# Moving the result's store to ScalarE, and the first load ahead of SyncE's base-address read

## The chip, the cores and the metric

The kernel runs on one core of one Trainium2 chip. The metric is the device time of one execution, in microseconds (us). Before the change it was 188.28 us (median of 3 runs, 188.20 to 188.41). A run's time is about 1.3 us longer than the span that its profile shows (187.95 against 186.69 us in the profiled run of before), because the span counts only from the first to the last recorded instruction of the kernel.

Names of engines: PE is TensorE's matmul, PEld its weight load, DVE is VectorE, ACT is ScalarE, POOL is GpSimd, SP is SyncE. "SPq" and "ACTq" are the sequencers of SyncE and ScalarE, which issue DMAs.

## The reference, cut

One decode step for 2 batch rows of 640 features: attention over the last 1024 entries of a 4096-entry cache (32 heads of 192), then a gated feed-forward block, both modulated by vectors made from `c`.

```python
mod = (_silu(c) @ w_mod).reshape(c.shape[0], 6, 1, -1)
sa, ca, ga, sb, cb, gb = (mod[:, i].copy() for i in range(6))   # written out in the original
h = _layernorm(x, axis=-1) * (1 + ca) + sa
x = x + ga * _A_ref(h, A_k_cache, A_v_cache, A_wq, A_wo)
h = _layernorm(x, axis=-1) * (1 + cb) + sb
x = x + gb * _B_ref(h, B_w_gate, B_w_up, B_w_down)
return x                                                        # (2, 1, 640) bf16: 2.5 KB
```

It reads 76.9 MB and writes 2.5 KB.

## The kernel before

All work is written as operations with reads and writes, and a small scheduler turns these into semaphore waits. Every weight and cache load is issued by SyncE, in the order of use. Two places matter here.

The end. The result lies in 8 rows of `finb`, 16 partitions apart (four chunks of 160 features, times two batch rows). SyncE stores them, and then waits for the store to land:

```python
S.op("pe", f, ..., name="down%d" % ci)               # last matmuls, per landed piece of w_down
S.op("dve", ... fin = ps * modR[:, 5], name="gb_y")
S.op("dve", ... finb = fin + X, name="outR")
S.dma("sp", k_dma(out[:, 0, :].rearrange("b (i n) -> i b n", i=NR), finb[0:P:RB, :]),
      sem_out, reads=["finb"], name="st_out")
# ... cut ...
S.emit("sp", nc.sync, tail=lambda e: e.wait_ge(sem_out, 16))
```

The beginning. A program starts with a preamble (zeroing of registers, a read of the core's base address into two registers on each engine, constants on GpSimd) and a barrier of all engines, which for each engine is a drain and a wait. The kernel before already lifts its first load, of `w_mod`, out of the body and puts it directly in front of SyncE's drain:

```python
body = nc.main_func.blocks[0].instructions
entry = next(i for i, x in enumerate(body) if x.opcode == "Drain" and x.engine == mybir.EngineType.SP)
first = S.lists["sp"].pop(0)                          # the load of w_mod
# ... cut: an assert ...
n0 = len(body)
first.fn(nc.sync).then_inc(first.sem, first.inc)
moved = body[n0:]
del body[n0:]
body[entry:entry] = moved
```

## Time and profile before

| what | value |
|---|---|
| time, span | 188.28 us, 186.7 us |
| chain of work that ended last | 72% DMA, 16% VectorE |
| DMA engines' busy share, each fortieth of the span | 8 to 9 tenths, all but the last |
| first load issued, second load issued | 0.00 and 0.79 us |
| end of outR to end of the span | 1.78 us |

From the page of the kernel before: the span, the row of DMA busy shares in tenths over 40 slices, and the chain's shares by engine.

```profile
span 186.7 us, 2408 instructions
...
DMA  8989998999999999999999999999999999999991
...
DMA 72%; DVE 16%; PE 5%; ACT 2%; SPq 1%; issue 1%
```

The DMA engines are busy for 80% or more of every slice until the last. This is a kernel that streams its weights and caches. Nothing at its two ends can matter unless it moves the whole stream (the head) or what follows the stream (the tail).

The timeline of before at the head. The columns are start (us), duration (us), engine, line, operation, output and input, count, and in brackets the idle time before it and what ended that.

```profile
0.00 0.39 SPq L266 DMA_DIRECT2D r<-in_w_mod_dram  x1
0.29 0.10 POOL L724 MEMSET const-float32-0.0<- 128x1 f32 x1 [0.29 <-issue]
...
0.79 0.81 SPq L266 DMA_DIRECT2D ring<-in_A_wq_dram  x2
```

The first load is the first thing recorded. The memset on GpSimd belongs to the preamble, and the load starts 0.295 us ahead of it. The second load comes after the barrier.

The timeline of before at the tail.

```profile
183.54 0.64 PE L684 MATMUL ps<-r,aT 128*17 128x160 bf16 x16 [0.65 <-DMA r<-in_B_w_down_dram]
...
184.23 0.33 DVE L689 TENSOR_TENSOR fin<-ps,modR 128x160 f32<-128x160 f32 x1 [2.73 <-PE ps L684]
184.59 0.33 DVE L691 TENSOR_TENSOR finb<-fin,X 128x160 bf16<-128x160 f32 x1
184.94 0.69 SPq L266 DMA_DIRECT2D out_dram<-finb  x1
```

And the waits of SyncE's queue in before: who waited for whom, us in total, times, the longest.

```profile
SPq L266 <- DVE finb L691: 23.3, 1, 23.3
...
SPq L706 <- DMA out_dram<-finb: 1.0, 1, 1.0
```

The last piece of `w_down` lands, 16 matmuls finish the product, two VectorE operations make the result, and then come 0.69 us of issuing and 1.0 us of waiting for 2.5 KB. No other work is left at that time, so this 1.7 us is wholly on the critical path.

### The profile page before, as it was taken

How to read it: one execution, taken by the hardware profiler on the slowest of the kernel's cores; microseconds unless marked ns; L12 is line 12 of the kernel's file. 1: busy time of each engine (PE TensorE's matmuls, PEld its weight loads, DVE VectorE, ACT ScalarE, POOL GpSimd, SP SyncE). 2: the span in 40 equal slices, each digit the busy share in tenths (PEclk: the TensorE clock that was granted, in tenths of full speed). 3: DMA queues.
4: the chain of work that ended last, by engine and by line, in shares of the span. 5: the costliest groups of instructions: out<-in, count | busy, mean ns of one | idle time of the engine just before them, and what ended most of it. 6: DMA issues, size and time to landing. Idle time of an engine off the chain costs nothing.

```text
span 186.7 us, 2408 instructions
## 1 busy us (share of the span) xinstructions
PE 106.9 (57%) x1038; PEld 51.9 (28%) x1039; DVE 98.2 (53%) x147; ACT 30.0 (16%) x72; POOL 5.1 (3%) x23
## 2 busy tenths in 40 slices
PE   0015710833876678656649656665576895356472
PEld 0011200211243333322314313333233252355321
DVE  6114000019788889587596595785865934002311
ACT  2022100091020212021012011110110103100610
POOL 8200000000000000000000000000000000000000
PEclk9999999997899999999996999999998558555567
DMA  8989998999999999999999999999999999999991
GB/s 296 486 366 437 474 422 379 437 427 427 429 424 427 417 426 432 424 424 425 421 427 427 427 430 421 420 429 424 429 422 424 449 462 422 404 402 428 408 399 51
DMA packets 6518, 77.03 MB, mean 413 GB/s; under 512 B 746, under 2 KB 876, under 8 KB 1516
## 3 DMA queue, kind: packets, MB, share of 16 engines
q1 hardware_dynamic: 6492, 76.88, 97.6%
q8 instruction: 8, 0.13, 0.3%
q14 instruction: 2, 0.02, 0.0%
q10 hardware_dynamic: 16, 0.01, 0.0%
HBM read 76.88 MB, written 0.00 MB: 412 GB/s over the span
## 4 chain that ended last, share of the span: by engine, by line
DMA 72%; DVE 16%; PE 5%; ACT 2%; SPq 1%; issue 1%
DMA ring<-in_A_k_cache_dram 38%; DMA ring<-in_A_wq_dram 17%; DMA r<-in_B_w_down_dram 17%; DVE prod L490 10%; DVE S_sb L509 4%; PE ps L502 2%; PE ps L467 2%; ACT qbc L483 2%; SPq L266 1%; DVE ps L485 1%; DVE M L512 1%; ACT qrow L474 1%; DVE bcR L519 0%; PE ps L526 0%; PE ps L684 0%
## 5 line engine op out<-in xcount | busy, mean ns | idle before, releaser
L490 DVE TENSOR_TENSOR prod<-ring,qbc 128x3072 bf16<-128x3072 bf16 x32 | 55.9, 1752 | 16.1 <-DMA ring<-in_A_k_cache_dram 16.1
L502 PE MATMUL ps<-prod,ident_b 128*128 128x512 bf16 x192 | 51.5, 411 | 15.7 <-DVE prod L490 15.6
L502 PEld LDWEIGHTS ps<-prod,ident_b 128*128 128x128 bf16 x192 | 17.2, 102 | 40.3 <-DVE prod L490 21.0
L509 DVE TENSOR_REDUCE S_sb<-ps 128x32 f32<-128x1024 f32 x16 | 19.3, 1206 | 0.9 <-PE ps L502 0.9
L526 PE MATMUL ps<-bcR,bcL 5*128 5x4 f32 x32 | 6.3, 264 | 22.3 <-DVE bcR L519 22.3
L563 ACT ACTIVATE On<-ps,rden 128x384 bf16<-128x384 f32 x16 | 9.3, 581 | 42.4 <-DVE rden L561 31.9
L551 PE MATMUL ps<-ring,E_sb 128*8 128x384 bf16 x256 | 14.8, 356 | 0.0
L534 ACT ACTIVATE E_sb<-Sb_sb 128x128 bf16<-128x128 f32 x16 | 5.0, 311 | 57.6 <-DVE Sb_sb L531 57.6
L467 PE MATMUL ps<-ring,hT 128*2 128x512 bf16 x60 | 6.7, 626 | 9.9 <-DMA ring<-in_A_wq_dram 9.0
L526 PEld LDWEIGHTS ps<-bcR,bcL 5*128 5x128 f32 x32 | 4.9, 190 | 26.3 <-DVE bcR L519 26.3
L622 PE MATMUL ps<-ring,oT 128*17 128x160 bf16 x192 | 6.8, 338 | 5.5 <-DMA ring<-in_A_wo_dram 5.5
L477 DVE CAST qrow<-ps 128x512 bf16<-128x512 f32 x1 | 0.7, 692 | 15.8 <-PE ps L467 15.8
L531 DVE TENSOR_TENSOR Sb_sb<-S_sb,ps 128x128 f32<-128x128 f32 x16 | 4.6, 289 | 7.8 <-PE ps L526 7.8
L540 PEld LDWEIGHTS ps<-denp,maskc 128*128 128x128 f32 x32 | 6.9, 218 | 3.6 <-ACT E_sb L534 0.9
L622 PEld LDWEIGHTS ps<-ring,oT 128*17 128x17 bf16 x192 | 6.1, 135 | 6.1 <-DMA ring<-in_A_wo_dram 6.1
L641 DVE TENSOR_TENSOR lnt<-ps,modR 128x160 f32<-128x160 f32 x1 | 0.3, 325 | 13.6 <-PE ps L622 13.6
L551 PEld LDWEIGHTS ps<-ring,E_sb 128*8 128x8 bf16 x256 | 5.0, 87 | 3.2 <-issue 0.7
L467 PEld LDWEIGHTS ps<-ring,hT 128*2 128x2 bf16 x60 | 1.7, 114 | 14.9 <-DMA ring<-in_A_wq_dram 9.9
L540 PE MATMUL ps<-denp,maskc 128*128 128x1 f32 x32 | 5.0, 226 | 0.8 <-ACT E_sb L534 0.8
L383 PE MATMUL ps<-ident_b,crow 2*128 2x2 bf16 x5 | 0.4, 177 | 8.2 <-DMA crow<-in_c_dram 8.2
L576 PE MATMUL ps<-On,zsel 128*128 128x96 bf16 x64 | 4.6, 223 | 0.7 <-ACT On L563 0.7
L514 PE MATMUL ps<-ident_f,M 128*1 128x128 f32 x16 | 4.5, 280 | 0.4 <-DVE M L512 0.4
(81 smaller groups left out, 71.5 us busy)
## 6 DMA issues: line engine op xcount, KB each, us to landing
ring<-in_A_k_cache_dram SPq DMA_DIRECT2D x16, 1536.0 KB, 24.6
ring<-in_A_v_cache_dram SPq DMA_DIRECT2D x16, 1536.0 KB, 24.8
r<-in_w_mod_dram SPq DMA_DIRECT2D x1, 4800.0 KB, 14.1
ring<-in_A_wq_dram SPq DMA_DIRECT2D x1, 4608.0 KB, 32.0
ring<-in_A_wo_dram SPq DMA_DIRECT2D x1, 4480.0 KB, 24.6
ring<-in_A_wq_dram SPq DMA_DIRECT2D x1, 3072.0 KB, 20.6
ring<-in_A_wo_dram SPq DMA_DIRECT2D x1, 2720.0 KB, 23.0
r<-in_B_w_gate_dram SPq DMA_DIRECT2D x1, 1920.0 KB, 25.1
```

Source lines behind the costliest of these rows:

```text
L467: last = e.matmul(ps[32 * i:32 * i + B, n, :], lhsT=hT[:, k, :], rhs=wv[:, kk, i, n * QW:(n + 1) * QW], start=(k == 0), stop=(k == KT - 1) ...
L490: S.op("dve", lambda e: e.tensor_tensor(out=prod[:, 2 * (g % 2) + ci, :, :], in0=ring[:, sl, ci * JC * Dh:(ci + 1) * JC * Dh].rearrange("p ...
L502: last = e.matmul(o_ap, lhsT=ident_b[:, :], rhs=prod[:, pz, :, t * GC:(t + 1) * GC], start=(t == 0), stop=(t == NCH - 1))
L509: S.op("dve", lambda e: e.tensor_reduce(out=S_sb[:, z, :], in_=ps[:, 2 * z:2 * z + 2, :].rearrange("p k (j c) -> p (k j) c", c=GC), axis=A ...
L526: S.op("pe", lambda e: e.matmul(ps[:, BK_T, P:P + HQ], lhsT=bcL[:, :], rhs=bcR[:, z, :], start=True, stop=True), reads=[("bcR", z), "bcL"] ...
L531: S.op("dve", lambda e: e.tensor_tensor(out=Sb_sb[:, z, :, :], in0=S_sb[:, z, :].unsqueeze(2).broadcast_to([P, J, HQ]), in1=ps[:, BK_T, P: ...
L534: S.op("act", lambda e: e.activation(out=E_sb[:, z, :, :], in_=Sb_sb[:, z, :, :], func=ACTF.Exp, scale=SCALE, accum_out=denp[:, z:z + 1]), ...
L540: S.op("pe", lambda e: e.matmul(ps[:, BK_T, P + 16:P + 17], lhsT=maskc[:, :], rhs=denp[:, z:z + 1], start=True, stop=True), reads=[("denp" ...
L551: last = e.matmul(ps[32 * i:32 * i + 2 * HQ, BK_O, 0:ON], lhsT=E_sb[:, z, 2 * jp:2 * jp + 2, :].rearrange("p j h -> p (j h)"), rhs=ring[:, ...
L563: S.op("act", lambda e: e.activation(out=On[:, quad % 2, b, :], in_=ps[:, BK_O, 0:ON], func=ACTF.Identity, scale=rden[:, z:z + 1]), reads= ...
L576: last = e.matmul(ps[:, BK_OT, 0:B * NT].rearrange("p (b t) -> p b t", b=B), lhsT=zsel[:, jj, x:x + P], rhs=On[:, quad % 2, :, jj * Dh + d ...
L622: last = e.matmul(ps[32 * i:32 * i + RM, BK_M, 0:DR], lhsT=oT[:, t, :], rhs=wv[:, tl, i, :], start=(t == 0), stop=(t == NT - 1), tile_posi ...
```

## The change

Its intent: ScalarE is idle at the end and could issue the store faster or sooner; and the very first load should not wait for the base-address read.

```diff
-        S.dma("sp", k_dma(out[:, 0, :].rearrange("b (i n) -> i b n", i=NR), finb[0:P:RB, :]),
+        S.dma("act", k_dma(out[:, 0, :].rearrange("b (i n) -> i b n", i=NR), finb[0:P:RB, :]),
               sem_out, reads=["finb"], name="st_out")
 
         S.resolve()
         body = nc.main_func.blocks[0].instructions
-        entry = next(i for i, x in enumerate(body) if x.opcode == "Drain" and x.engine == mybir.EngineType.SP)
+        own = [i for i, x in enumerate(body) if x.engine == mybir.EngineType.SP]
+        entry = next(i for i in own if body[i].opcode == "Drain")
+        base = next(i for i in own if body[i].opcode == "ISA")
+        assert base < entry
+        body.insert(entry - 1, body.pop(base))
+        entry -= 1
```

In the source, SyncE's order becomes: first load, base-address read, drain. It was: base-address read, first load, drain.

## The prediction

> **What bounds the kernel now.** The page: span 186.7 us (that run took 187.95; median 188.28). Its row of DMA busy shares is 8 or 9 tenths in every slice but the last; the chain that ended last is 72% DMA. So it is a streaming kernel, and this change touches only its two ends.
>
> Head (timeline): SyncE issues the w_mod load at 0.00, the next load at 0.79, after the entry barrier; w_mod has landed at 14.1 and PE uses it at 14.16. A real advance of the first load could save as much as it advances, since everything queues behind it.
>
> Tail (timeline and DMA packets): the last w_down load lands at 183.5, the last matmuls end at 184.2, outR ends at 184.91, SyncE issues the store from 184.94 to 185.63, its packets run at 186.23 to 186.33, the last completion increment is at 186.66, SyncE's final wait is over at 186.68. The store's issue and landing, 1.72 us, lie wholly on the critical path.
>
> **The entry part.** The base-address read is an instruction of the common preamble that writes two registers. Nothing in this program reads them. In the compiled program of the kernel before, SyncE's stream holds no such read: the w_mod load is its first kernel instruction, then the drain and the barrier's wait. The unused read is dropped on compiling, and should be dropped wherever it stands. I expect a stream equal to the one before, and 0.00 us here. If the read did survive, moving it would be worth at most its own duration, which the trace does not show.
>
> **The store.** Removed: SyncE's issue, 694 ns. Added: the same issue on ScalarE, 8 rows of 320 bytes. The trace has a near twin: ScalarE's load of x, the same shape the other way, 630 ns; its first completion count (written when issuing is done) came 1.06 us after the issue began, the store's on SyncE 1.07 us. Waking on VectorE takes ScalarE 33 to 36 ns, SyncE 27 to 29: +6 ns. ScalarE is idle from 178.4, SyncE from 161.6, so nothing is freed. SyncE still waits for the store to land. The Trainium skill, "DMA: Bandwidth & Descriptors", section "Issuing engines are not separate DMA queues", says that issuing elsewhere saves only sequencer time and that all transfers share 16 engines; the trace agrees: ScalarE's two small loads at the head, issued at 0.80 and 1.40, landed at 8.2 and 12.5, behind SyncE's packets. At the tail the DMA engines are empty. Unknown: from issue's end to first packet SyncE's store took 0.60 us; for ScalarE's queue, idle since 12 us, there is no clean figure. Sum: -0.06 to +0.2 us, about +0.02.
>
> **Prediction.** 188.25 us, 187.85 to 188.7 at 8 in 10 (mostly spread between executions and chips). Faster by over 2%: 0.005; within 2%: 0.985; slower by over 2%: 0.01.
>
> **What would show it.** First load at 0.00, SyncE's second load at about 0.79, PE's mod matmuls at about 14.2; the store issued by ScalarE about 35 ns after outR, for 0.60 to 0.72 us, on the queue that carried c and x; end of outR to end of span 1.65 to 1.95 us (before: 1.78).
>
> **What would make it wrong.** The read survives and costs some tenths at the start; ScalarE's long idle queue starts late; ScalarE's end-of-program work, now begun about 7 us later, outlasts SyncE's final wait and lengthens the time outside the span (1.26 us in the profiled run).

## The result, and the profile after

| | before | after |
|---|---|---|
| median | 188.16 us (6 runs, 187.88 to 188.41) | 188.21 us (6 runs, 188.14 to 188.32) |
| span of the profiled run | 186.69 us | 186.89 us |
| its time less its span | 1.257 us | 1.256 us |

The ratio is 1.0004, with a 95% interval of 0.9991 to 1.0017: the same. (A ratio here and below is the mean time of one kernel's fast runs over that of the other's of the same rounds, so it is not quite the ratio of the medians quoted beside it.)

The page of after, the same three lines.

```profile
span 186.9 us, 2409 instructions
...
DMA  9989999999999999999999999999999999999991
...
DMA 72%; DVE 16%; PE 6%; ACT 2%; SPq 1%; issue 1%
```

The timeline of after at the head.

```profile
0.00 0.37 SPq L266 DMA_DIRECT2D r<-in_w_mod_dram  x1
0.29 0.10 POOL L729 MEMSET const-float32-0.0<- 128x1 f32 x1 [0.29 <-issue]
...
0.79 0.80 SPq L266 DMA_DIRECT2D ring<-in_A_wq_dram  x2
```

Nothing has moved: the first load is 0.295 us ahead of the memset, exactly as before. The reason is seen in the compiled program. This is SyncE's stream from its start, in before and in after alike:

```
DMACopy         r3 <- w_mod
Drain           (entry barrier)
EventSemaphore  (entry barrier)
DMACopy         ring <- wq
```

There is no base-address read in either. Nothing in the program reads the two registers that it fills, and it is dropped when the program is built. Instruction by instruction, SyncE's two compiled streams differ in one thing: the store at the end is gone.

The timeline of after at the tail, and the wait of SyncE's queue for the store.

```profile
184.47 0.33 DVE L689 TENSOR_TENSOR fin<-ps,modR 128x160 f32<-128x160 f32 x1 [2.78 <-PE ps L684]
184.83 0.33 DVE L691 TENSOR_TENSOR finb<-fin,X 128x160 bf16<-128x160 f32 x1
185.19 0.60 ACTq L266 DMA_DIRECT2D out_dram<-finb  x1
```

```profile
SPq L711 <- DMA out_dram<-finb: 25.3, 1, 25.3
```

The store is now ScalarE's, 0.09 us shorter to issue. SyncE's wait has grown from 1.0 to 25.3 us, which looks alarming and costs nothing: SyncE had nothing else to do, and it used to spend the first 23.3 us of that time waiting for VectorE instead. (This shows why a sum of waits is no measure of cost. What counts is when the last one ends.)

The tail in detail, from the instruction, packet and semaphore records of the trace, in us after the end of outR:

| | issue starts | issue lasts | first completion count | first packet | last completion count | span ends |
|---|---|---|---|---|---|---|
| before (SyncE) | 0.028 | 0.694 | 1.100 | 1.321 | 1.747 | 1.780 |
| after (ScalarE) | 0.033 | 0.603 | 1.058 | 1.273 | 1.708 | 1.741 |

ScalarE wakes 5 ns later, issues 91 ns shorter, and its first packet then follows 0.637 us after the end of the issue in place of 0.599: the gain is 39 ns of 188 us. The span of this after run is nevertheless 0.20 us longer, all of it between the memset and the end of outR, where the two programs do the same; between executions of one program that stretch varies as much (store_only, below, compiles to the same program as after, byte for byte, and its span is 0.31 us shorter; entry_only compiles to that of before and its span is 0.11 us longer).

The first completion count is worth a look. The Trainium skill, "DMA: Bandwidth & Descriptors", section "Why a DMA increments its semaphore by 16 and not by 1", says that such a transfer uses k of 16 DMA engines, k being the largest number up to 16 that divides the slowest dimension of both sides, and that the sequencer writes the missing 16 - k at once while each used engine adds one when its data has landed. This store's dimensions are 8 on one side and 4 on the other, so k should be 4, and the trace agrees: until the span's end its semaphore has five updates, in before as in after: one early, and about 0.6 us later four within 45 to 49 ns.

### The profile page after: what moved, and what is told of

Same layout as the page of the kernel before. It is cut to its first block, busy times and chain, and to the rows that moved or that the text cites. A ratio compares the mean times of both kernels' runs of the same rounds, so it can differ in the third digit from the quotient of the medians.

```text
span 186.9 us, 2409 instructions
## 1 busy us (share of the span) xinstructions
PE 105.3 (56%) x1039; PEld 51.3 (27%) x1039; DVE 98.0 (52%) x147; ACT 29.9 (16%) x72; POOL 5.1 (3%) x23
## 4 chain that ended last, share of the span: by engine, by line
DMA 72%; DVE 16%; PE 6%; ACT 2%; SPq 1%; issue 1%
DMA ring<-in_A_k_cache_dram 38%; DMA ring<-in_A_wq_dram 17%; DMA r<-in_B_w_down_dram 17%; DVE prod L490 10%; DVE S_sb L509 4%; PE ps L502 2%; PE ps L467 2%; ACT qbc L483 2%; SPq L266 1%; DVE ps L485 1%; DVE M L512 1%; PE ps L526 0%; DVE bcR L519 0%; PE ps L684 0%; ACT qrow L474 0%
## 5 line engine op out<-in xcount | busy, mean ns | idle before, releaser
L502 PE MATMUL ps<-prod,ident_b 128*128 128x512 bf16 x192 | 49.2, 396 | 16.3 <-DVE prod L490 16.2
L445 PE MATMUL ps<-r,scT 128*17 128x480 bf16 x40 | 4.3, 598 | 2.1 <-DMA r<-in_w_mod_dram 2.1
L519 DVE TENSOR_REDUCE bcR<-ps 1x4 f32<-1x128 f32 x16 | 4.3, 272 | 0.8 <-PE ps L514 0.8
## 6 DMA issues: line engine op xcount, KB each, us to landing
r<-in_B_w_gate_dram SPq DMA_DIRECT2D x1, 1920.0 KB, 25.3
```

Source lines behind the costliest of these rows:

```text
L502: last = e.matmul(o_ap, lhsT=ident_b[:, :], rhs=prod[:, pz, :, t * GC:(t + 1) * GC], start=(t == 0), stop=(t == NCH - 1))
```

## The experiments

My theory: the entry part compiles to nothing; the store's issue and landing are on the critical path, but cost the same to within 0.1 us on either engine. Rivals: (a) the two parts each move time and cancel; (b) the head or the tail has slack, so that such changes could not matter; (c) ScalarE's later finish lengthens the end of the program. Rival (c) is answered by the result itself: the time outside the span is 1.257 us before and 1.256 us after in the profiled runs.

### 1. Each part alone

Two kernels, `entry_only` (the diff without its store line) and `store_only` (the store line alone).

> Only the entry part of the change. The compiled program is byte for byte that of the kernel before. Mine: a null test, within 0.15 us of the kernel before, and any difference is the spread between executions. Rival (the entry part gains something and the store gives it back): faster by 0.2 us or more, the first load earlier against the first memset than the 0.29 us of before.

> Only the store moved to ScalarE. Mine: within 0.15 us of before; from the end of outR to the end of the span 1.70 to 1.80 us (before 1.78, with both parts 1.74). Rival (the two parts cancel): slower by 0.2 us or more, with a longer time outside the span than 1.26 us.

`entry_only`: 188.12 us against 188.27, ratio 0.9996 (0.9983 to 1.0010). The first load lies 0.294 us ahead of the memset, and the end of outR to the end of the span is 1.782 us. As the compiled programs are byte for byte the same on all five engines, this is what no change looks like: two medians 0.15 us apart.

`store_only`: 188.03 us, ratio 0.9993 (0.9980 to 1.0005). The end of outR to the end of the span is 1.745 us, its issue 0.612 us, close to the changed kernel. Its tail:

```profile
184.51 0.33 DVE L691 TENSOR_TENSOR finb<-fin,X 128x160 bf16<-128x160 f32 x1
184.87 0.61 ACTq L266 DMA_DIRECT2D out_dram<-finb  x1
```

So the parts do not cancel (rival a): one is nothing and the other is 0.04 us. That figure comes from the traces, where five runs with the old store show 1.776 to 1.792 us and two with ScalarE's show 1.741 and 1.745; the times alone cannot resolve it.

### 2. The base-address read, kept alive

What would the entry part be worth if the read did run? One instruction that stores its register into an unused word, placed where SyncE idles, keeps it in the program. `live_ahead` adds this to the kernel before, `live_behind` to the kernel with the entry part.

```diff
+        junk = sb("junk", [1, 2], mybir.dt.int32)
...
+        keep = _Op("sp", lambda e: e.reg_save(junk[0:1, 0:1], e.tpb_base_reg.lo), "keep_base")
+        S.lists["sp"].insert(len(S.lists["sp"]) - 1, keep)      # ahead of the store
```

(The function that emits the operations also got three lines that emit this one without a semaphore.)

> The base-address read is kept in the program by one later store of its register into an unused word (issued while SyncE idles), and it stands ahead of the first load, as the source of the kernel before has it. Mine: the read now runs, delays the first load by its own duration d, and the whole program by d, since all loads queue behind the first: slower than before by d, which I estimate at 0.05 to 0.6 us; the first load comes later against the first memset than in before. Rival (the head has slack): the first load is later but the time is the same.

> The same live read, standing behind the first load, as the changed source has it. Mine: within 0.15 us of before, faster than live_ahead by nearly all of d, as the read hides behind the first load's transfer; the second load may come later by d without cost. Rival (the read costs the same wherever it stands, as the second load and the entry barrier follow it): as slow as live_ahead.

The timeline of live_ahead at the head.

```profile
0.06 0.38 SPq L270 DMA_DIRECT2D r<-in_w_mod_dram  x1
0.28 0.10 POOL L730 MEMSET const-float32-0.0<- 128x1 f32 x1 [0.28 <-issue]
...
0.84 0.81 SPq L270 DMA_DIRECT2D ring<-in_A_wq_dram  x2
```

And of live_behind.

```profile
0.00 0.39 SPq L270 DMA_DIRECT2D r<-in_w_mod_dram  x1
0.29 0.10 POOL L735 MEMSET const-float32-0.0<- 128x1 f32 x1 [0.29 <-issue]
...
0.84 1.07 SPq L270 DMA_DIRECT2D ring<-in_A_wq_dram  x2
```

Now the trace holds the read, an instruction recorded as a base load: at 0.000 us in live_ahead, with the first load 64 ns later, and at 0.457 us in live_behind. In live_ahead the load is 0.215 us ahead of the memset in place of 0.295. Placed behind, the load is back at 0.293 and it is the barrier that is late: the second load stands 0.55 us after the memset in place of 0.50. That costs nothing visible, since the DMA engines have w_mod's 4800 KB to move until about 14 us.

The times: live_ahead 188.31 us, ratio 1.0007 (0.9995 to 1.0020); live_behind 188.24 us, ratio 1.0003 (0.9990 to 1.0015). Both are the same as before; 0.06 to 0.08 us is at the lower edge of what I had expected and too little for the times to show. So the order of the first load and the read is worth at most 0.08 us even in a program in which the read exists. That the total gains this much from moving it stays argued, not measured.

### 3. Does the head have slack?

`late_first` leaves out the lifting altogether: the first load is an ordinary instruction after the barrier (the nine lines from `body = ...` on are deleted).

> The first load is issued after the entry barrier, not ahead of it. In before it starts 0.29 us ahead of the first memset on GpSimd; here it should start 0.35 to 0.50 us after that memset, a delay of 0.64 to 0.79 us. Mine (everything queues behind the first load, so the head is fully on the critical path): slower than before by 0.6 to 0.8 us, ratio 1.003 to 1.0045. Rival (the head has slack, which is why the entry part did nothing): within 0.15 us.

Its timeline at the head.

```profile
0.30 0.10 POOL L715 MEMSET const-float32-0.0<- 128x1 f32 x1 [0.30 <-issue]
...
0.80 0.39 SPq L266 DMA_DIRECT2D r<-in_w_mod_dram  x1
...
1.25 0.88 SPq L266 DMA_DIRECT2D ring<-in_A_wq_dram  x2
```

The load starts 0.492 us after the memset in place of 0.295 ahead of it: 0.787 us later. The second load, behind it on SyncE, starts 0.45 us later than in before. The time is 188.97 us against 188.30, ratio 1.0033 (1.0020 to 1.0045), which is 0.62 us of 188.3. So the head has no slack worth speaking of (rival b falls there), and the first load's place is a real lever. The kernel before had pulled it already; the change had nothing left to pull.

### 4. Does the tail have slack?

The store cut in two, one per batch row, both issued by ScalarE (`split_act`), or one by SyncE and one by ScalarE (`split_sp_act`):

```diff
-        S.dma("sp", k_dma(out[:, 0, :].rearrange("b (i n) -> i b n", i=NR), finb[0:P:RB, :]),
-              sem_out, reads=["finb"], name="st_out")
+        for bb, eng in ((0, "act"), (1, "act")):                 # split_sp_act: "sp" for row 0
+            S.dma(eng, k_dma(out[bb, 0, :].rearrange("(i n) -> i n", i=NR), finb[RB * bb:RB * bb + 97:32, :]),
+                  sem_outs[bb], reads=["finb"], name="st_out%d" % bb)
...
-        S.emit("sp", nc.sync, tail=lambda e: e.wait_ge(sem_out, 16))
+        S.emit("sp", nc.sync, tail=lambda e: [e.wait_ge(s, 16) for s in sem_outs])
```

> The store is cut in two, one for each batch row, both issued by ScalarE one after the other; SyncE waits for both. Mine (the issue of the store is fully on the critical path): a second issue of about 0.6 us is added, end of outR to end of span 2.3 to 2.45 us against 1.74 with one store on ScalarE, and slower than before by 0.5 to 0.65 us. Rival (issuing overlaps with the landing, so its engine and its length do not matter): within 0.15 us.

> The same two stores, one issued by SyncE and one by ScalarE at the same time. Mine: the issue is mostly a fixed cost, so each half takes about 0.6 us and the two run side by side: end of outR to end of span 1.65 to 1.80 us, within 0.15 us of before. If the issue scaled with the rows it would be 1.4 us and 0.3 us faster. Rival (two issuing engines get in each other's way): 2.0 us or more.

The tail of split_act (two issues merged in one line).

```profile
184.95 0.32 DVE L691 TENSOR_TENSOR finb<-fin,X 128x160 bf16<-128x160 f32 x1
185.31 1.11 ACTq L266 DMA_DIRECT2D out_dram<-finb  x2
```

Two issues of 0.568 and 0.512 us follow each other, and the end of outR to the end of the span grows to 2.242 us, 0.50 us more than with one store on ScalarE. The time is 188.78 us against 188.30, ratio 1.0021 (1.0009 to 1.0034), or 0.40 us (0.17 to 0.64). A little less than I had expected, since the halves are shorter to issue, but clear: the tail has no slack either (rival b falls there too).

The tail of split_sp_act.

```profile
184.81 0.32 DVE L691 TENSOR_TENSOR finb<-fin,X 128x160 bf16<-128x160 f32 x1
185.16 0.66 SPq L266 DMA_DIRECT2D out_dram<-finb  x1
185.16 0.57 ACTq L266 DMA_DIRECT2D out_dram<-finb  x1
```

Here my expectation failed. The two issues start within 4 ns of each other and look parallel. ScalarE's half lands as it does alone (first count 1.02, last 1.66 us after outR). SyncE's half has its first count at 1.38 us and its last at 2.01 us, with an issue of 0.657 us that is not longer than usual. The span ends 2.03 us after outR, later than with one store (1.78). The time is 188.50 us, ratio 1.0008 (0.9996 to 1.0021), the same within the noise. Against the same two halves issued one after the other (split_act, 2.24 us), issuing at once did save 0.21 us, but that is far from the 0.60 us by which the second issue there starts after the first. So the two issues seem to have got in each other's way somewhere between the sequencers and the DMA engines, after the recorded issue; the order of the two first packets (ScalarE's at 1.25, SyncE's at 1.60 us, on engines otherwise idle) suggests that it was not the DMA engines. What they share there, these runs do not show, and this is one trace; no run issues SyncE's half alone (its whole stores with this partition step, in six traces, have their first count at 1.09 to 1.12 us).

### 5. If not the engine, the shape

The trace of before has issues of two lengths on SyncE. Where its queue is not full, plain two-dimensional loads take 0.33 to 0.43 us, the cache loads and the store 0.53 to 0.69 us (0.63 and more at the head and for the store). On ScalarE, the load of x takes 0.63 us, and the plain load of c 0.55. (The expectation below says 0.61 to 0.69 us for the long ones; most of the cache loads take 0.53 to 0.54.) `rows_flat` stores 8 neighbouring partitions in plain order. Its result is wrong (the result does not lie there); the bytes and rows are as many.

```diff
-        S.dma("sp", k_dma(out[:, 0, :].rearrange("b (i n) -> i b n", i=NR), finb[0:P:RB, :]),
+        S.dma("sp", k_dma(out[:, 0, :].rearrange("b (i n) -> (b i) n", i=NR), finb[0:2 * NR, :]),
               sem_out, reads=["finb"], name="st_out")
```

> A deliberately wrong result: SyncE stores the first 8 partitions, whose addresses form a plain two-dimensional block on both sides, in place of the 8 rows that lie 16 partitions apart. Same bytes, same rows. The trace has two lengths of issue: 0.33 to 0.43 us for plain two-dimensional loads, 0.61 to 0.69 us for those with a third dimension. Mine: the issue takes 0.33 to 0.43 us, end of outR to end of span 1.40 to 1.55 us, faster than before by 0.2 to 0.35 us: the shape of the store is worth more than its engine. Rival: the issue is as long as before, 0.6 us or more, and the time the same.

Its tail.

```profile
184.84 0.33 DVE L691 TENSOR_TENSOR finb<-fin,X 128x160 bf16<-128x160 f32 x1
185.20 0.37 SPq L266 DMA_DIRECT2D out_dram<-finb  x1
```

The issue takes 0.368 us in place of 0.694, and the first packet follows 0.421 us after it in place of 0.599. The end of outR to the end of the span is 1.286 us, 0.49 us less than before and more of a gain than I had expected (1.40 to 1.55). The time is 187.70 us against 188.30, ratio 0.9966 (0.9952 to 0.9979), which is 0.64 us (0.40 to 0.90). The 0.49 us of the tail are more than ten times what the engine is worth there.

Which property of the shape does it? `stride_rows` (also wrong) keeps two plain dimensions and 8 rows on both sides, but reads `finb[0:P:RB, :]` again, 16 partitions apart.

> A deliberately wrong result: the store reads the 8 rows 16 partitions apart, as before, but writes them to the output in plain order, so both sides have two dimensions and only the partition step is left of what made the store different from rows_flat. Mine: the compiler marks rows_flat's store for the shorter issue and not this one, so the issue is 0.6 to 0.7 us again and the end of outR to the end of the span 1.65 to 1.80 us. Rival (the third dimension of the output side, or 8 rows shared out over 8 DMA engines in place of 4, made rows_flat short): 1.25 to 1.45 us.

```profile
184.75 0.32 DVE L691 TENSOR_TENSOR finb<-fin,X 128x160 bf16<-128x160 f32 x1
185.10 0.71 SPq L266 DMA_DIRECT2D out_dram<-finb  x1
```

The issue is 0.714 us, the first packet 0.597 us after it, the end 1.805 us after outR, the time 188.11 us (ratio 0.9999, 0.9987 to 1.0012). So neither the third dimension nor the number of DMA engines used (both wrong-result stores have nine semaphore updates, which is k = 8) makes the store short. With two plain dimensions on both sides, neighbouring partitions do. (They are not enough alone: the cache loads write 128 neighbouring partitions, have a third dimension on the other side, and are long.) In the compiled programs the short store and all of SyncE's short loads carry a mark for a prepared form of issue, and the long ones do not. (ScalarE's load of c carries it too and still took 0.55 us, so the mark does not explain every length.)

### 6. A correct version with the short store

`gather` pays for neighbouring partitions with a matmul. A 0/1 matrix gathers the 8 rows of gb*y, rounded to bf16 here, into partitions 0 to 7, in the output's order; X is gathered in the same way earlier, beside the stream.

```diff
-        fin = sb("fin", [P, DR], F32)
-        finb = sb("finb", [P, DR], BF16)
+        fin = sb("fin", [P, DR], BF16)
+        finb = sb("finb", [B * NR, DR], BF16)      # also new: selo, selof (0/1, made on GpSimd), Xg
...
+        S.op("pe", lambda e: e.matmul(ps[0:B * NR, 3, 0:DR], lhsT=selof[:, :, :].rearrange("p b i -> p (b i)"), rhs=X[:, :], ...
+        S.op("dve", lambda e: e.tensor_copy(out=Xg[:, :], in_=ps[0:B * NR, 3, 0:DR]), ...      # both after the gate matmuls
...
-        S.op("dve", lambda e: e.tensor_tensor(out=finb[:, :], in0=fin[:, :], in1=X[:, :], op=ALU.add), ...
-        S.dma("sp", k_dma(out[:, 0, :].rearrange("b (i n) -> i b n", i=NR), finb[0:P:RB, :]), ...
+        S.op("pe", lambda e: e.matmul(ps[0:B * NR, 3, 0:DR], lhsT=selo[:, :, :].rearrange("p b i -> p (b i)"), rhs=fin[:, :], ...
+        S.op("dve", lambda e: e.tensor_tensor(out=finb[:, :], in0=ps[0:B * NR, 3, 0:DR], in1=Xg[:, :], op=ALU.add), ...
+        S.dma("sp", k_dma(out[:, 0, :].rearrange("b (i n) -> (b i) n", i=NR), finb[:, :]), ...
```

> A correct version with rows_flat's store: one matmul with a 0/1 matrix gathers the 8 rows of gb*y into 8 neighbouring partitions in the output's order, X is gathered the same way earlier, and outR adds the two. Added on the critical path: one weight load and matmul of 160 columns and its hop, estimated from the aT step and the transposes at 0.25 to 0.35 us; taken away: 0.49 us of the store. Mine: faster than before by 0.10 to 0.30 us; start of gb_y to end of span 2.15 to 2.35 us against 2.47 before. If the added hop costs as much as the store saves: the same within 0.1 us.

> The same with the store issued by ScalarE. Mine: within 0.1 us of gather, the end of outR to the end of the span within 0.1 us of gather's 1.29 or so: the engine matters as little for the short store as for the long one. Rival (ScalarE's advantage of 0.04 us was a property of the long issue): up to 0.2 us slower than gather.

The tail of gather.

```profile
184.16 0.32 DVE L700 TENSOR_TENSOR fin<-ps,modR 128x160 bf16<-128x160 f32 x1 [2.79 <-PE ps L695]
...
184.54 0.29 PE L702 MATMUL ps<-fin,selo 128*8 128x160 bf16 x1 [0.43 <-DVE fin L700]
184.87 0.31 DVE L704 TENSOR_TENSOR finb<-ps,Xg 8x160 bf16<-8x160 f32 x1 [0.38 <-PE ps L702]
185.21 0.37 SPq L269 DMA_DIRECT2D out_dram<-finb  x1
```

From the start of gb_y to the end of the span is 2.302 us, against 2.466 in before: the store gives back 0.50 us, the hop through PE takes 0.34. The outputs are right. The time is 187.83 us against 188.08, ratio 0.9987 (0.9973 to 1.0001). With the store on ScalarE (`gather_act`) it is 187.93 us, ratio 0.9988 (0.9976 to 1.0001): the issue is 0.312 us in place of 0.367, the first packet comes 0.479 us later in place of 0.427, and the end of outR to the end of the span is 1.286 us against 1.280. ScalarE issues shorter here too, and here too what follows takes it back.

As that interval just reached 1, gather ran once more:

> The gather version once more, as its interval (0.9973 to 1.0001) just reaches 1. The traces put its tail, from the start of gb_y to the end of the span, at 2.31 us against 2.47 before, so mine: 0.10 to 0.30 us faster than before, ratio 0.9984 to 0.9995. If the first result was luck of the chip: ratio 0.9995 to 1.0005.

187.98 us against 188.05, ratio 0.9995 (0.9981 to 1.0009), with 2.306 us from gb_y to the end. The three ratios give 0.24, 0.23 and 0.09 us, and the traces 0.16 us each time. I take 0.16 us as what the tail gains. That gather beats the kernel before as a whole is likely, but its times do not prove it.

## Why the prediction was right

- The time: 188.25 us predicted, 188.21 measured; within 2%, as said. This alone tests little, since 2% is 3.8 us, and 0.04 us is less than the spread of the runs. What tests the account are the two ends in the traces.
- The entry part at 0.00 us: right and for the reason given. The read is in neither compiled program; it comes back as soon as something reads its register (live_ahead), which shows that its absence is a matter of the missing reader. "At most its own duration" holds only if the time to the next issue is counted in: the load moves by 0.06 to 0.08 us, while the read itself is recorded with 0.012 us in live_ahead (0.102 in live_behind).
- "A real advance of the first load could save as much as it advances": late_first turned it round, 0.79 us of delay for 0.62 us of time (0.38 to 0.85 by its interval).
- The store: predicted to start about 35 ns after outR and to last 0.60 to 0.72 us, measured 33 ns and 0.603. End of outR to end of span predicted 1.65 to 1.95, measured 1.741. The sum was put at -0.06 to +0.2 us, about +0.02, and is -0.04: inside the range, with the other sign than its middle. The twin used for the estimate, ScalarE's load of x at 0.630 us, was a good one.
- PE's first modulation matmuls were to stay at about 14.2 us; they came at 14.38, and at 13.99 to 14.20 in the two single-part kernels. This mark moves with the landing of w_mod from run to run and is too coarse to test a change of tenths.
- Of the things that would have made it wrong, one half happened: ScalarE's queue did start later after its issue, by 0.038 us, and took back part of the 0.091 us. That its queue had been idle long is not the reason: in split_act the second store, issued right behind the first, has its first packet 0.649 us after its issue, the first one 0.638.

What the prediction did not see is where the tail's time could be had: in the shape of the store's source rather than in the engine that issues it. Both lengths of issue stood in the trace of before.

## What to carry to other kernels

Before ordering instructions by hand, look whether they are in the compiled program at all, and find a mark in the trace (here a memset of the preamble) against which a shift would show. The last transfer was on the critical path here with its issue and its landing; moving it to another idle engine left both in place, and the engine's name was worth 0.04 us here, while the shape of the access was worth 0.49. When a change is worth less than the spread of the times, its own stretch in the trace (here from the end of outR to the end of the span, repeatable to 0.02 us) measures what the times cannot.

## What the Trainium skill lacked or had wrong

- "DMA: Bandwidth & Descriptors", section "Issuing engines are not separate DMA queues", says that issuing on several engines at once saves only the sequencers' time for issuing. In split_sp_act it saved only a part of that: two half stores issued at once by SyncE and ScalarE ended 2.03 us after outR, against 2.24 us when ScalarE issued both in turn with 0.60 us between their starts. SyncE's half had its first completion count at 1.38 us in place of about 1.1.
- The same page, section "Latency and other measured facts", gives one figure for the first byte of a DMA issued by SyncE or ScalarE, about 600 ns. The traces show 0.60 (SyncE) and 0.64 us (ScalarE) from the end of a long issue, but 0.42 to 0.43 and 0.48 us for the short form, and from the start of the issue 1.24 to 1.31 us and 0.79 us.
- No page says that the trn2 issue has a short and a long form, or that an SBUF side with a step between partitions makes it long: on SyncE 0.367 us against 0.69 to 0.71 us for 8 rows of 320 bytes, and 0.49 us in all to the landing.
- None has the base-address read, or that it is dropped when nothing reads its registers: 64 ns from its start to the next issue where it is kept.
